# Spreading VectorE's work over ScalarE, GpSimd and TensorE, and giving 160 rows of w2 to five DMA engines

## The chip, the core and the metric

The kernel runs on one core of a Trainium2 chip. The metric is the device time of one execution in microseconds; the median of three runs before the change is 344.48 us (344.46 to 344.8).

## What is computed

One decode step for two sequences: an attention block and a small feed-forward block on the same input, mixed by a gate.

```python
g = sigmoid((x * gate_w).sum(-1, keepdims=True))          # x: [2, 1, 512]
q = (x @ wq)                                              # 32 heads of 128
scores = einsum("bhqd,bhkd->bhqk", q, k_cache) * 128**-0.5  # k_cache: [2, 32, 4096, 128]
o = einsum("bhqk,bhkd->bhqd", softmax(scores), v_cache)
a = o.reshape(2, 1, 4096) @ wo                            # wo: [4096, 512]
b = relu(x @ w1) @ w2                                     # w1: [512, 1376], w2: [1376, 512]
out = g * a + (1 - g) * b
```

Everything is bf16. The two caches are 67 MB each, all inputs together 145.4 MB, and each byte is read once.

## The kernel before

SBUF holds three regions of 8 MB (`kv`, NREG = 3). K and V are each cut into eight units of 8 MB, eight heads of one sequence to a unit. The list `order` gives the order in which units are loaded: K0 to K4, V0, K5, V1, K6, V2, K7, then V3 to V7. Unit n goes into region n modulo 3, so its transfer waits until the unit three places earlier has been used (`freed`). All big transfers are issued by SyncE (SP) in this order (L216 to L242): wq and w1 first, into the third region, then the units, then the two halves of wo (L232) and the four parts of w2 (w2a L236; w2b, w2c, w2d L239), and at last the output. V7 comes in two parts, v7a and v7b. x and gate_w are loaded on ScalarE's queue. A transfer over 128 rows of SBUF is split over sixteen DMA engines, eight rows each; each engine counts the transfer's semaphore up by one when its part has landed, and the waiting engine waits for sixteen.

Each compute engine has a list of operations written out by hand (`_Prog`), and a marker (`signal`) per operation that others can wait for (`waits`). For each K unit VectorE turns the unit in 32 x 32 blocks, in four steps (`k_turn`, L360), and TensorE then multiplies it, 64 matmuls in four steps `rp`, with a padded copy of q (`wz`, written by `w_block` on ScalarE, L351) into four PSUM banks (`k_scores`, L365 and L393). After four units one sequence's scores are complete: VectorE takes the maximum (`sm_max`, L399 to L410), ScalarE the exponentials (`sm_exp`, L414), VectorE turns them (`sm_turn`, L422). For each V unit GpSimd spreads the probabilities into `ptm` (`spread`, L431), TensorE multiplies them with the unit (`v_unit`, 64 matmuls, L448), VectorE masks the result and sums its four column blocks (`v_extract`, L455 and L459), and TensorE adds it into the sequence's output (`v_gather`, L464). `o_denominator` (L470, L473), `o_scale` (L476) and `o_place` (L484, L489) finish the attention; `project` (L500) multiplies it with wo and the hidden layer with w2, in steps of four matmuls in the order in which the weights land, and two engines copy the result out of PSUM (L510).

The gate, the projection of q and the hidden layer h (`gate`, `q_proj`, `ffn_h`, L281 to L343) run at the start, while K0 is being loaded.

## Time and profile before

| | before |
|---|---|
| median of 3 runs | 344.48 us |
| the profiled execution: its own time, its span | 344.46 us, 343.1 us |
| DMA: bytes, mean rate over the span | 145.59 MB, 424 GB/s |
| TensorE matmuls busy | 179.8 us (52%) |
| VectorE busy | 169.7 us (49%) |
| GpSimd busy, ScalarE busy | 35.5 us (10%), 13.5 us (4%) |
| chain that ended last, by engine | DMA 57%, VectorE 24%, TensorE 9%, issue 4% |

The span is the stretch that the profile covers; the execution's own time is 1.36 us longer. Rows of the profile count from the span's start. A group's row gives the line, the engine, the operation, its tiles, how often it ran, and then its busy time and the mean duration of one. PE is TensorE, DVE VectorE, ACT ScalarE, POOL GpSimd, SPq the queue of SyncE. A row of the chain gives start, length and what it was. The trace also holds a record of each DMA packet (start, duration, bytes, queue), but not which of the sixteen engines moved it.

### The profile page before, as it was taken

What the parts mean: (1) busy time and instruction counts of PE and PEld (TensorE: products, weight loads), DVE (VectorE), ACT (ScalarE), POOL (GpSimd) and SP (SyncE); (2) the same over time, 40 slices, a digit from 0 to 9 for tenths busy, and PEclk for the clock granted to TensorE, in tenths of its full rate; (3) what the DMA queues carried; (4) which work ended last, traced back from release to release, by engine and by line L of the source; (5) the groups of instructions that cost most, each with busy time, mean ns of one, the idle gap of its engine ahead of it and who ended that gap; (6) DMA issues with size and microseconds to landing.
All of it is one profiled execution on the core that took longest, in us unless ns stands there. A gap on an engine that the chain in (4) does not pass through costs nothing.

```text
span 343.1 us, 2541 instructions
## 1 busy us (share of the span) xinstructions
PE 179.8 (52%) x1322; PEld 39.6 (12%) x938; DVE 169.7 (49%) x87; ACT 13.5 (4%) x44; POOL 35.5 (10%) x50
## 2 busy tenths in 40 slices
PE   0510196996869409935980099205970503307353
PEld 0210000100001000120120011100020201102122
DVE  0210797979899489439910694219935020102020
ACT  1010001000010110000000000000020000000000
POOL 3000000000000040040013000400004040403100
PEclk9965599899989957995995579955996575856586
DMA  8998989999999989898999989999999999999995
GB/s 325 451 483 374 481 374 481 397 458 420 435 460 390 489 382 474 382 468 390 466 466 391 481 384 466 405 451 405 460 405 443 466 392 474 413 401 449 395 428 216
DMA packets 3588, 145.59 MB, mean 424 GB/s; under 512 B 405, under 2 KB 634, under 8 KB 890
## 3 DMA queue, kind: packets, MB, share of 16 engines
q1 hardware_dynamic: 3572, 145.43, 98.5%
q8 instruction: 9, 0.15, 0.2%
q10 hardware_dynamic: 6, 0.00, 0.0%
q14 instruction: 1, 0.01, 0.0%
HBM read 145.43 MB, written 0.00 MB: 424 GB/s over the span
## 4 chain that ended last, share of the span: by engine, by line
DMA 57%; DVE 24%; PE 9%; issue 4%; another core or an unknown queue 3%; SPq 1%; ACT 1%
DMA kv<-in_A_k_cache_dram 34%; DVE kv L360 22%; DMA kv<-in_B_w_dram 13%; DMA kv<-in_A_v_cache_dram 11%; PE PS L365 4%; PE PS L448 4%; PE PS L393 2%; DVE E L422 1%; ACT E L414 1%; DVE mpad L399 1%; DVE X L459 0%; SPq L232 0%; DVE X L455 0%; PE PS L500 0%
## 5 line engine op out<-in xcount | busy, mean ns | idle before, releaser
L360 DVE STREAM_TRANSPOSE kv<-kv 128x4096 uint32<-128x4096 uint32 x32 | 139.3, 4412 | 50.2 <-DMA kv<-in_A_k_cache_dram 50.2
L365 PE MATMUL PS<-kv,wz 128*128 128x512 bf16 x384 | 114.0, 407 | 0.0
L393 PE MATMUL PS<-kv,wz 128*128 128x512 bf16 x128 | 52.9, 413 | 94.5 <-DVE kv L360 94.4
L431 POOL TENSOR_TENSOR ptm<-E,mask 128x512 bf16<-128x512 bf16 x32 | 32.2, 1039 | 282.2 <-DVE E L422 158.5
L448 PE MATMUL PS<-kv,ptm 128*32 128x512 bf16 x512 | 38.6, 462 | 36.3 <-DMA kv<-in_A_v_cache_dram 36.3
L455 DVE TENSOR_TENSOR X<-PS,maskc 128x512 f32<-128x512 f32 x8 | 5.5, 687 | 79.4 <-PE PS L448 79.4
L393 PEld LDWEIGHTS PS<-kv,wz 128*128 128x128 bf16 x128 | 13.0, 102 | 206.2 <-DVE kv L360 120.6
L448 PEld LDWEIGHTS PS<-kv,ptm 128*32 128x32 bf16 x512 | 17.5, 113 | 54.3 <-issue 47.2
L351 ACT ACTIVATE wz<-q_sb 32x8 bf16<-32x8 bf16 x32 | 6.9, 214 | 154.5 <-PE PS L365 145.6
L464 PE MATMUL PS<-X,selx 128*32 128x128 f32 x16 | 3.5, 302 | 13.3 <-DVE X L459 13.3
L459 DVE TENSOR_REDUCE X<-X 128x128 f32<-128x512 f32 x8 | 8.2, 1024 | 0.3
L399 DVE TENSOR_REDUCE mpad<-PS 128x2 f32<-128x2048 f32 x2 | 4.6, 2292 | 7.5 <-PE PS L365 7.5
L414 ACT ACTIVATE E<-PS,negm 128x1024 bf16<-128x1024 f32 x4 | 4.4, 1109 | 81.8 <-DVE negm L410 81.8
L422 DVE STREAM_TRANSPOSE E<-E 128x2048 bf16<-128x2048 bf16 x2 | 4.6, 2312 | 4.7 <-ACT E L414 4.7
L312 PE MATMUL PS<-kv,xT 128*32 128x512 bf16 x32 | 3.6, 629 | 3.6 <-DMA kv<-in_A_wq_dram 3.6
L500 PE MATMUL PS<-kv,oW 128*2 128x128 bf16 x128 | 2.9, 264 | 4.5 <-DMA kv<-in_A_wo_dram 4.5
L510 DVE CAST ptm<-PS 2x128 bf16<-2x128 f32 x2 | 0.6, 280 | 9.1 <-PE PS L500 9.1
L319 DVE STREAM_TRANSPOSE ptm<-PS 128x1024 f32<-128x1024 f32 x1 | 1.3, 1251 | 6.3 <-PE PS L312 6.3
L286 DVE COPY xT<-PS 128x8 bf16<-128x8 bf16 x1 | 0.2, 164 | 8.1 <-PE PS L284 8.1
L510 ACT ACTIVATE ptm<-PS 2x128 bf16<-2x128 f32 x2 | 0.5, 270 | 84.0 <-PE PS L500 84.0
L464 PEld LDWEIGHTS PS<-X,selx 128*32 128x32 f32 x16 | 1.1, 112 | 19.0 <-DVE X L459 15.7
L500 PEld LDWEIGHTS PS<-kv,oW 128*2 128x2 bf16 x128 | 2.5, 102 | 4.8 <-DMA kv<-in_A_wo_dram 4.2
(56 smaller groups left out, 24.2 us busy)
## 6 DMA issues: line engine op xcount, KB each, us to landing
kv<-in_A_v_cache_dram SPq DMA_DIRECT2D x1, 6144.0 KB, 47.8
kv<-in_A_wq_dram SPq DMA_DIRECT2D x1, 4096.0 KB, 12.2
kv<-in_A_wo_dram SPq DMA_DIRECT2D x2, 2048.0 KB, 40.1
kv<-in_A_v_cache_dram SPq DMA_DIRECT2D x1, 2048.0 KB, 52.3
kv<-in_B_w_dram SPq DMA_DIRECT2D x1, 1376.0 KB, 15.0
kv<-in_B_w_dram SPq DMA_DIRECT2D x1, 640.0 KB, 43.4
kv<-in_B_w_dram SPq DMA_DIRECT2D x1, 512.0 KB, 44.2
kv<-in_A_k_cache_dram SPq DMA_DIRECT2D x8, 40.2
```

Source lines behind the costliest of these rows:

```text
L351: act(lambda e, a=a: e.activation(out=wz[32 * a:32 * a + 32, u % 2, :, 31 + 32 * a:33 + 32 * a], in_=q_sb[32 * a:32 * a + 32, b, ub].rearr ...
L360: dve(lambda v, rp=rp: v.transpose(out=reg[:, 4096 * rp:4096 * (rp + 1)], in_=reg[:, 4096 * rp:4096 * (rp + 1)]), dwaits=([landed(what)] i ...
L365: return e.add_instruction(mybir.InstMatmult(name=nc.get_next_instruction_name(), engine=mybir.EngineType.PE, ins=[e.lower_ap(rhs), e.lowe ...
L393: return e.matmul(dst, lhsT=w, rhs=m, start=first, stop=final, skip_group_check=True)
L399: dve(lambda v: v.tensor_reduce(out=mpad[:, 0:2], in_=PSF[:, 0:2048].rearrange("p (x h q) -> p h x q", h=2, q=16), axis=AX.XY, op=ALU.max) ...
L414: act(lambda a, h=h: a.activation(out=E[:].rearrange("p (x h q) -> p h x q", h=2, q=16)[:, h], in_=PSF[:, 0:2048].rearrange("p (x h q) -> ...
L422: dve(lambda v: v.transpose(out=E[:], in_=E[:]), waits=[f"act_exp{b}"], signal=f"dve_et{b}")
L431: pool(lambda g, src=src, dst=dst: g.tensor_tensor(out=dst, in0=src, in1=msk, op=ALU.mult), waits=([f"dve_et{b}", "dve_mask8"] + ([f"pe_v_ ...
L448: pe(lambda e, ci=ci, t=t: e.matmul(psf(32 * t, 32 * t + 32, c0, 512), lhsT=ptm[:, ci].rearrange("p c h -> p (c h)"), rhs=rows[:, 512 * ci ...
L455: dve(lambda e: e.tensor_tensor(out=X2[:].rearrange("p (c d) -> p c d", c=4), in0=psf(0, 128, c0, 512).rearrange("p (c d) -> p c d", c=4), ...
L459: dve(lambda e: e.tensor_reduce(out=X3[:], in_=X2[:].rearrange("p (c d) -> p d c", c=4), axis=AX.X, op=ALU.add), waits=[f"dve_x_{v}"] + ([ ...
L500: pe(lambda e, t=t, n=n, w=w, m=m: e.matmul(psf(32 * t, 32 * t + 2, FIN_C0, 128), lhsT=w, rhs=m[:, 128 * t:128 * t + 128], start=(n == 0), ...
```

## The change

1. The rows of w2 are dealt anew. 160 rows (`w2p`) are loaded by eight transfers of five SBUF rows each, 4 KB a row, issued ahead of wo (the change's own words put them on the DMA engines 0 to 4); w2a has 64 rows instead of 96, w2b 640 as before, w2c 384 instead of 512, w2d 128 as before. The hidden layer is cut to match, in 14 blocks instead of 11.
2. Work moves off VectorE. To ScalarE: the copies of x and q, parts of the gate, relu of h, the scaling of the maximum, the copy of V's products out of PSUM (except for V7), the last copy of the attention's output. To GpSimd: the mask on V's products, and `w_block`, now one multiplication instead of four ScalarE activations per unit. To TensorE: the gate's product, and the sum over V's four column blocks: `v_gather` takes 512 columns and adds all units of a sequence, and VectorE sums the four blocks once per sequence in `o_scale`.
3. A K unit is turned in two steps instead of four. The first half of K4 is turned ahead of the first softmax, the second half behind it.
4. GpSimd clears one tile (`zero`) instead of eight, the masks are made in fewer steps, `o_denominator` runs once for both sequences.
5. The first half of wo is multiplied by 32 matmuls of 64 x 256 instead of 64 of 2 x 128.

In the built programs VectorE has 44 instructions instead of 109, ScalarE 32 instead of 47, GpSimd 65 as before, SyncE 38 instead of 30.

```diff
-    w2_sb = kv[:, WO, 16384:22016].rearrange("p (r n) -> p r n", n=512)
-
-    act(lambda e: e.dma_start(x_sb, A_x.rearrange("b s d -> (b s) d")).then_inc(sem["x"], 16))
-    act(lambda e: e.dma_start(gw_sb, gate_w.rearrange("(o d) -> o d", o=1)).then_inc(sem["gw"], 16))
+    w2_sb = kv[:, WO, 16384:23552].rearrange("p (r n) -> p r n", n=512)
+    W2 = (("w2p", 0, 4, 0, 40), ("w2a", 160, 1, 4, 64), ("w2b", 224, 5, 5, 128), ("w2c", 864, 3, 10, 128), ("w2d", 1248, 1, 13, 128))
...
+    for j in range(8):
+        sp(lambda e, j=j: e.dma_start(w2_sb[j:40:8, 0:4, :].rearrange("p r n -> p (r n)"),
+                                      B_w2[0:160, :].rearrange("(p r) n -> p (r n)", r=4)[j::8]).then_inc(sem["w2p"], 16),
+           waits=([freed(order[wo_reg - NREG])] if j == 0 else []))
     for x in range(2):
         sp(lambda e, x=x: e.dma_start(wo_sb[:, x * 8192:(x + 1) * 8192],
                                       A_wo[x * 2048:(x + 1) * 2048, :].rearrange("(p r) n -> p (r n)", p=128))
-           .then_inc(sem[f"wo{x}"], 16), waits=([freed(order[wo_reg - NREG])] if x == 0 else []))
-
-    sp(lambda e: e.dma_start(w2_sb[0:96, 10, :], B_w2[1280:1376, :]).then_inc(sem["w2a"], 16))
-    W2 = (("w2b", 0, 5, 0), ("w2c", 640, 4, 5), ("w2d", 1152, 1, 9))
-    for name, row, n, r0 in W2:
+           .then_inc(sem[f"wo{x}"], 16))
+
+    sp(lambda e: e.dma_start(w2_sb[0:64, 4, :], B_w2[160:224, :]).then_inc(sem["w2a"], 16))
+    for name, row, n, r0, _ in W2[2:]:
         sp(lambda e, name=name, row=row, n=n, r0=r0: e.dma_start(
             w2_sb[:, r0:r0 + n, :].rearrange("p r n -> p (r n)"),
             B_w2[row:row + 128 * n, :].rearrange("(p r) n -> p (r n)", p=128)).then_inc(sem[name], 16))
...
-        dve(lambda v: v.tensor_copy(out=xT[:], in_=PSB[0:128, XT_B0:XT_B0 + 8].rearrange("p (t b) -> p t b", t=4)),
-            waits=["pe_xT"], signal="dve_xT0")
-        dve(lambda v: v.tensor_copy(out=xT32[:, :, 0:2], in_=PSB[0:128, XT_B0:XT_B0 + 8].rearrange("p (t b) -> p t b", t=4)),
-            waits=["c_x32"], signal="dve_x32")
...
-        dve(lambda v: v.tensor_tensor(out=xg[:], in0=xT[:], in1=gwT[:].unsqueeze(2).to_broadcast([128, 4, 2]), op=ALU.mult),
-            waits=["dve_xT"], signal="dve_xg")
-        dve(lambda v: v.tensor_reduce(out=xgs[:], in_=xg[:].rearrange("p t b -> p b t"), axis=AX.X, op=ALU.add),
-            waits=["dve_xg"], signal="dve_xgs")
-        pe(lambda e: e.matmul(psf(0, 128, G_C0, 2), lhsT=ones, rhs=xgs[:, :], start=True, stop=True),
-           waits=["dve_xgs", "c_ones"], signal="pe_z")
+            pe(lambda e, t=t: e.matmul(psf(0, 128, G_C0, 2), lhsT=xT32[:, t, 2:3].to_broadcast([128, 128]), rhs=xT32[:, t, 0:2],
+                                       start=(t == 0), stop=(t == 3)),
+               waits=(["act_xT"] if t == 0 else []), signal=("pe_z" if t == 3 else None))
...
-        dve(lambda v: v.tensor_copy(out=q_sb[:].rearrange("p b u h k -> p b (u h k)"),
-                                    in_=qt.rearrange("p (n x) -> p x n", x=32)[:, 0:2]),
-            waits=["dve_qt"], signal="dve_q")
+        act(lambda a: a.activation(out=q_sb[:].rearrange("p b u h k -> p b (u h k)"),
+                                   in_=qt.rearrange("p (n x) -> p x n", x=32)[:, 0:2], func=ACT.Copy),
+            waits=["dve_qt"], signal="act_q")
...
-            dve(lambda v, b=b: v.tensor_scalar(out=hT[:, 0:10, b], in0=PSF[:, H_C0 + b:H_C0 + 20:2], scalar1=0.0,
-                                               scalar2=gm[:, b:b + 1], op0=ALU.max, op1=ALU.mult),
-                waits=["pe_h", "dve_gm"])
-            dve(lambda v, b=b: v.tensor_scalar(out=hT[0:96, 10, b:b + 1], in0=psf(0, 96, H_C0 + 20 + b, 1), scalar1=0.0,
-                                               scalar2=gm[0:96, b:b + 1], op0=ALU.max, op1=ALU.mult),
-                signal=f"dve_h{b}")
+            act(lambda a, b=b: a.activation(out=hT[:, :, b], in_=PSF[:, H_C0 + b:H_C0 + 2 * NF:2], func=ACT.Relu,
+                                            scale=gm[:, b:b + 1]),
+                waits=["pe_h"] + ([] if b else ["act_gm"]), signal=f"act_h{b}")
...
-        for a in range(4):
-            act(lambda e, a=a: e.activation(out=wz[32 * a:32 * a + 32, u % 2, :, 31 + 32 * a:33 + 32 * a],
-                                            in_=q_sb[32 * a:32 * a + 32, b, ub].rearrange("p h k -> p k h"), func=ACT.Copy),
-                 waits=((["dve_q", "c_wz"] if u < 2 else [f"pe_sc_{u - 2}"]) if a == 0 else []),
...
+        out = wz[:, u % 2].rearrange("p k c -> p k c")[:, :, 31:159].rearrange("p k (a x) -> p k a x", a=4)[:, :, :, 0:2]
+        q = q_sb[:, b, ub].rearrange("p h k -> p k h").unsqueeze(2).to_broadcast([128, 4, 4, 2])
+        msk = mask4[:].unsqueeze(1).unsqueeze(3).to_broadcast([128, 4, 4, 2])
+        pool(lambda g: g.tensor_tensor(out=out, in0=q, in1=msk, op=ALU.mult),
+             waits=([["act_q", "dve_mask8"], []] + [[f"pe_sc_{x}"] for x in range(6)])[u], signal=f"pool_wz{u}")
...
-        for rp in range(4):
-            dve(lambda v, rp=rp: v.transpose(out=reg[:, 4096 * rp:4096 * (rp + 1)], in_=reg[:, 4096 * rp:4096 * (rp + 1)]),
-                dwaits=([landed(what)] if rp == 0 else []), signal=f"dve_kt_{u}_{rp}")
+        for h in halves:
+            dve(lambda v, h=h: v.transpose(out=reg[:, 8192 * h:8192 * (h + 1)], in_=reg[:, 8192 * h:8192 * (h + 1)]),
+                dwaits=([landed(what)] if h == 0 else []), signal=f"dve_kt_{u}_{h}")
...
-                    if blk == 0 and rb == 0:
-                        waits = [f"dve_kt_{u}_{rp}"]
+                    if blk == 0 and rb == 0 and rp % 2 == 0:
+                        waits = [f"dve_kt_{u}_{rp // 2}"]
                         if rp == 0:
-                            waits += [f"act_wz{u}"] + (["act_exp0"] if u == 4 else [])
+                            waits += [f"pool_wz{u}"] + (["act_exp0"] if u == 4 else [])
...
-        dve(lambda v: v.tensor_scalar(out=nrow[:].rearrange("p (u r h) -> p u r h", r=4, h=2),
-                                      in0=mmax[:].rearrange("p (u h) -> p u h", h=2).unsqueeze(2).to_broadcast([128, 4, 4, 2]),
-                                      scalar1=-INV_SQRT_DH, scalar2=None, op0=ALU.mult),
-            waits=[f"dve_mm{b}"], signal=f"dve_mn{b}")
-        dve(lambda v: v.transpose(out=negm[:, b, :], in_=nrow[:]), waits=[f"dve_mn{b}"], signal=f"dve_neg{b}")
+        act(lambda a: a.activation(out=nrow[:].rearrange("p (u r h) -> p u r h", r=4, h=2),
+                                   in_=mmax[:].rearrange("p (u h) -> p u h", h=2).unsqueeze(2).to_broadcast([128, 4, 4, 2]),
+                                   func=ACT.Copy, scale=-INV_SQRT_DH),
+            waits=[f"dve_mm{b}"], signal=f"act_mn{b}")
+        dve(lambda v: v.transpose(out=negm[:, b, :], in_=nrow[:]), waits=[f"act_mn{b}"], signal=f"dve_neg{b}")
...
-        dve(lambda e: e.tensor_tensor(out=X2[:].rearrange("p (c d) -> p c d", c=4),
-                                      in0=psf(0, 128, c0, 512).rearrange("p (c d) -> p c d", c=4),
-                                      in1=maskc[:].unsqueeze(2).to_broadcast([128, 4, 128]), op=ALU.mult),
-            waits=[f"pe_v_{v}"] + ([f"dve_y_{v - 1}"] if v else []), signal=f"dve_x_{v}")
-        dve(lambda e: e.tensor_reduce(out=X3[:], in_=X2[:].rearrange("p (c d) -> p d c", c=4), axis=AX.X, op=ALU.add),
-            waits=[f"dve_x_{v}"] + ([f"pe_g_{v - 1}"] if v else []), signal=f"dve_y_{v}")
...
+        if v == 7:
+            dve(lambda e: e.tensor_tensor(out=X, in0=src.rearrange("p (c d) -> p c d", c=4), in1=msk, op=ALU.mult),
+                waits=[f"pe_v_{v}"], signal=f"dve_x_{v}")
+            return
+        act(lambda e: e.activation(out=X2[:], in_=src, func=ACT.Copy), waits=[f"pe_v_{v}"], signal=f"act_x_{v}")
+        pool(lambda e: e.tensor_tensor(out=X, in0=X, in1=msk, op=ALU.mult),
+             waits=[f"act_x_{v}"] + ([] if v else ["dve_setup"]), signal=f"pool_x_{v}")
 
     def v_gather(v):
         b, ub = divmod(v, 4)
-        pe(lambda e: e.matmul(psf(0, 32, O_C0, 128), lhsT=selx[:, 24 - 8 * ub:56 - 8 * ub], rhs=X3[:],
+        pe(lambda e: e.matmul(psf(0, 32, O_C0, 512), lhsT=selx[:, 24 - 8 * ub:56 - 8 * ub], rhs=X2[:],
                               start=(ub == 0), stop=(ub == 3), skip_group_check=True),
-           waits=[f"dve_y_{v}", "dve_selx"] + (["dve_O0"] if v == 4 else ["dve_h1"] if v == 0 else []), signal=f"pe_g_{v}")
...
-    def o_denominator(b):
-        for h in range(2):
-            pe(lambda e, h=h: e.matmul(psf(0, 32, L_C0 + b, 1), lhsT=sell[:, h, :], rhs=lsum[:, b, h:h + 1],
-                                       start=(h == 0), stop=(h == 1), skip_group_check=True),
...
+    def o_denominator():
+        for b in range(2):
+            for h in range(2):
+                pe(lambda e, b=b, h=h: e.matmul(psf(0, 32, L_C0 + b, 1), lhsT=sell[:, h, :], rhs=lsum[:, b, h:h + 1],
+                                                start=(h == 0), stop=(h == 1), skip_group_check=True),
+                   waits=(["act_exp1", "dve_setup"] if b == 0 and h == 0 else []), signal=("pe_l" if b and h else None))
+        dve(lambda v: v.reciprocal(out=rinv[:], in_=psf(0, 32, L_C0, 2)), waits=["pe_l"], signal="dve_rinv")
 
     def o_scale(b):
-        dve(lambda v: v.tensor_scalar(out=O_sb[:, b, :], in0=psf(0, 32, O_C0, 128), scalar1=rinv[:, b:b + 1],
+        dve(lambda v: v.tensor_reduce(out=Osum[:], in_=psf(0, 32, O_C0, 512).rearrange("p (c d) -> p d c", c=4), axis=AX.X, op=ALU.add),
+            waits=[f"pe_g_{4 * b + 3}"], signal=f"dve_S{b}")
+        dve(lambda v: v.tensor_scalar(out=O_sb[:, b, :], in0=Osum[:], scalar1=rinv[:, b:b + 1],
                                       scalar2=gb[0:32, b:b + 1], op0=ALU.mult, op1=ALU.mult),
-            waits=[f"pe_g_{4 * b + 3}", f"dve_rinv{b}", "dve_g"], signal=f"dve_O{b}")
+            waits=[f"dve_S{b}"], signal=f"dve_O{b}")
...
-        dve(lambda v: v.tensor_copy(out=oW[:].rearrange("p (x r) c -> p x r c", x=2),
-                                    in_=psf(0, 128, R_C0, 64).rearrange("p (x b r) -> p x r b", x=2, b=2)),
-            waits=["pe_R"], signal="dve_oW")
+
+        R = psf(0, 128, R_C0, 64).rearrange("p (x b r) -> p x r b", x=2, b=2)
+        act(lambda a: a.activation(out=oW[:, 0:2], in_=R[:, 0:1].to_broadcast([128, 2, 16, 2]), func=ACT.Copy), waits=["pe_R"])
+        act(lambda a: a.activation(out=oW[:, 2], in_=R[:, 1], func=ACT.Copy), signal="act_oW")
...
-        steps = [(oW[:, r, :], wo_sb[:, r * 512:(r + 1) * 512]) for r in range(32)]
-        steps += [(hT[0:96, 10, :], w2_sb[0:96, 10, :])] + [(hT[:, r, :], w2_sb[:, r, :]) for r in range(10)]
-        lands = {0: "wo0", 16: "wo1", 32: "w2a", 33: "w2b", 38: "w2c", 42: "w2d"}
+        for r in range(16):
+            for g in range(2):
+                pe(lambda e, r=r, g=g: e.matmul(
+                    psf(64 * g, 64 * g + 64, FIN_C0 + 256 * g, 256),
+                    lhsT=oW[:].rearrange("p k r c -> p (k r c)")[:, 2 * r:2 * r + 64],
+                    rhs=wo_sb[:, r * 512 + 256 * g:r * 512 + 256 * g + 256], start=(r == 0), stop=False,
+                    tile_position=(0, 64 * g), skip_group_check=True),
+                   dwaits=([(sem["wo0"], 16)] if r == 0 and g == 0 else []),
+                   waits=(["act_oW", "act_h1", "act_exp1"] if r == 0 and g == 0 else []))
+        steps = [(hT[0:40, r, :], w2_sb[0:40, r, :]) for r in range(4)]
+        steps += [(oW[:, 2, r, :], wo_sb[:, 8192 + r * 512:8704 + r * 512]) for r in range(16)]
+        steps += [(hT[0:64, 4, :], w2_sb[0:64, 4, :])] + [(hT[:, r, :], w2_sb[:, r, :]) for r in range(5, NF)]
+        lands = {0: ("w2p", 128), 4: ("wo1", 16), 20: ("w2a", 16), 21: ("w2b", 16), 26: ("w2c", 16), 29: ("w2d", 16)}
         for n, (w, m) in enumerate(steps):
             for t in range(4):
-                pe(lambda e, t=t, n=n, w=w, m=m: e.matmul(psf(32 * t, 32 * t + 2, FIN_C0, 128), lhsT=w, rhs=m[:, 128 * t:128 * t + 128],
-                                                          start=(n == 0), stop=(n == len(steps) - 1), tile_position=(0, 32 * t),
-                                                          skip_group_check=True),
-                   dwaits=([(sem[lands[n]], 16)] if n in lands and t == 0 else []),
-                   waits=(["dve_oW", "dve_h1", "act_exp1"] if n == 0 and t == 0 else []),
+                pe(lambda e, t=t, n=n, w=w, m=m: e.matmul(psf(32 * t, 32 * t + 2, FIN_C0 + 128 * t, 128), lhsT=w,
+                                                          rhs=m[:, 128 * t:128 * t + 128], start=False, stop=(n == len(steps) - 1),
+                                                          tile_position=(0, 32 * t), skip_group_check=True),
+                   dwaits=([(sem[lands[n][0]], lands[n][1])] if n in lands and t == 0 else []),
                    signal=("pe_fin" if n == len(steps) - 1 and t == 3 else None))
...
+    k_turn(4, (0,))
     sm_max(0)
     sm_exp(0)
     sm_turn(0)
     spread(0)
-    k_turn(4)
+    k_turn(4, (1,))
     k_scores(4)
...
-    o_denominator(0)
     w_block(6)
     for v in range(8):
         v_unit(v)
+        if v == 3:
+            o_denominator()
...
-            o_denominator(1)
             o_scale(0)
...
```

## Prediction

> **What bounds the kernel now.** I read the page's row of DMA use first, then its rows of DMA queues, then the chain of waits from its end, then the trace's DMA packet records.

> ```profile
> DMA  8998989999999989898999989999999999999995
> ```
> ```profile
> q1 hardware_dynamic: 3572, 145.43, 98.5%
> q8 instruction: 9, 0.15, 0.2%
> ...
> q14 instruction: 1, 0.01, 0.0%
> ```
> ```profile
> 296.49 44.17 DMA kv<-in_B_w_dram
> 340.66 0.04 issue
> 340.71 0.64 PE PS L500 x18
> 341.35 0.02 issue
> 341.37 0.28 DVE ptm L510
> ```

> The sixteen DMA engines are never idle, and the chain ends on the last transfers of w2. So VectorE (49% of the span) and TensorE (52%) set nothing as long as no transfer is issued late; the end is set by the DMA engine that finishes last. The packet records give it: on one engine each packet starts 3 or 4 ns before the one ahead ends, so they string into sixteen chains without a hole from 1.77 us on. Seven chains end at 338.73 to 339.12, one at 339.90, eight at 340.20 to 340.57. All carry the same bytes. What differs is the 10 instruction packets of the second fence. Each of the eight late chains holds one 16 KB packet of q8 (22.9 to 336.4 us; the ninth comes at 340.45, behind all data): it takes 1.02 us and the data packet behind it 0.49 us longer than its like, 1.5 us in all. The chain of 339.90 holds q14's 8 KB packet (182.51 us; 0.30 and 0.65 us). TensorE starts 258 instructions on average from one q8 packet to the next, 64 bytes each, so q8 is its stream.

> [...]

> **w2 on five engines: the only part on the path.** An engine's share of w2 today is 6 packets of 1 KB (w2a), 8 of 5 KB (w2b), 8 of 4 KB (w2c), 8 of 1 KB (w2d). It becomes 4, 8, 8 of 3 KB, 8. In these chains 1 KB packets follow each other every 42.5 ns and 4 KB packets every 156 ns, so a KB more in a packet is 38 ns, and a 3 KB packet, which no row shows, lies between them at 118. Gone from every engine: 2 x 0.0425 + 8 x 0.038 = 0.39 us. Five engines get 8 packets of 4 KB and eight semaphore writes of 6 ns: 1.25 + 0.05 = 1.30, net +0.91.

> - An engine with a fetch: 340.57 - 0.39 = 340.18 at the latest.
> - One of the five, without a fetch: 339.12 + 0.91 = 340.03 at the latest.

> If the five are among the seven early ones, the last packet comes 0.39 us sooner. Behind it nothing changes: w2d lands 0.42 us after its last packet (340.99), its four matmuls end at 341.35, then two casts and the 2 KB write. w2c has 12 matmuls where it had 16.

> Are they among the seven? A row of x goes to each of two engines, and gate_w, one row, to one of these. The packets put the second of them into an early chain to the end; the first is lost where chains coincide within 1 ns. Eight fetches struck eight different engines, which drawing at random would do 1 time in 8, so they go in turn. If eight neighbours of sixteen take them and the second engine (number 1, if the two are 0 and 1) is free, four of the eight possible stretches leave 0 to 4 free; a turn over the upper eight alone, which eight fetches use up exactly, would leave them free too. So I put it somewhat above half.

> **VectorE's instructions.** Removed from it: 16 of 32 K turns (two of twice the size cost the same 17.4 us), gate, h, q and mask operations at 0.15 to 0.23 each, 8 reductions L459 (1.02) and 7 multiplications L455 (0.69). VectorE was not the bound, so this time is worth nothing. But in the built programs it falls from 109 instructions to 44, and q14's packet came with its 62nd, the 41st of GpSimd, the 16th of SP. If it is VectorE's, it goes; worth 0.95 us to an engine that is not last, hence nothing unless it is one of the five.

> **What is new on the waits.** All of this is costed at nothing; here is the cover.

> - K turns by halves: TensorE starts a half 4.4 us later and has 32 matmuls instead of 16 behind the last turn, 7.0 us for 3.5 (112.44 to 116.12 today). Each score unit ends 3.5 us later, and so does the issue that waits for it. Most issues have 12 to 31 us of queued transfers ahead of them. The tightest:

> ```profile
> 145.06 0.33 SPq L229 DMA_DIRECT2D kv<-in_A_v_cache_dram  x1
> ```

>   It waits for K unit 4. After the change: K4 lands at 114.44, half a turn ends at 123.3, softmax takes its 7.9 us (116.12 to 124.02 today) and 0.1 for ScalarE's step in it: 131.3; the other half 140.1; 32 matmuls 147.1. K5's first engine lands at 151.37, and 1.0 us goes from issue to first packet (wq: 0.74, 1.77), so the queue runs dry only from 150.4: 3.3 us to spare. After an idle stretch TensorE's first twelve matmuls stand 0.43 apart instead of 0.217 (from 128.41), which costs 2.6 of the 3.3 at most.
> - wz blocks on GpSimd: one multiplication instead of four activations (0.21 each). Nearest rows: 0.12 (small memset) to 1.04 (L431, sixteen times the elements); I take 0.2. They queue ahead of spread and behind score units that are done earlier; TensorE has two units in hand.
> - V's extract: a ScalarE copy of 512 columns (half of the 1.11 for 1024 at L414: 0.55) and a GpSimd multiplication (1.04 at L431 for as many elements; in f32 up to twice that) ahead of spread: 1.6 to 2.7 us on spread(7), which then ends at 320.4 to 321.5 (318.76 today), while v7a lands at 322.59; I take the lower, by the row of the same count.
> - Gather over 512 columns instead of 128: 0.41 becomes about 1.1. At the end: V7 done 328.65, multiplication 329.4, gather 330.5, reduction (1.02) 331.6, scale 332.0, place 332.6, ScalarE twice 333.2 where oW stood at 332.23. Then 32 matmuls of twice the width, 1.1 to 2.1 us: 335.3, while wo1 lands at 337.54. 2.2 us of cover; without it the end would move one for one.
> - SP issues eight more transfers at 0.43, 3.4 us, ahead of wo. wo0 was issued at 294.70 with 30.7 us queued.

> **Sum.** The profiled execution took 344.46 (span 343.1); 344.46 - 0.39 = 344.07; the median of the runs is 0.02 higher: 344.1.

> **Rivals.**
> 1. Slower: one or more of engines 0 to 4 takes a fetch. Then it ends at 340.20 to 340.57 plus 0.91, 0.54 to 0.91 later than today: 345.0 to 345.4, with several struck the upper end. It decides from the first of the five struck. Against it: the second engine's early chain. For it: nothing in the records names the other four. Chance 0.30.
> 2. The refill of q14 is not VectorE's, or is not lost, and falls to one of the five: 339.90 + 0.91 = 340.81, 0.24 later: 344.7. Chance 0.07.
> 3. The issue of V1 comes after 150.4. With all 32 matmuls at 0.43 (13.7 us) unit 4 ends at 153.8 and the end moves by 3.4: 347.9. Against it: from 133.2 they stand 0.217 apart. Chance 0.05.
> 4. The transfers don't go to five engines. All on one: 40 x 0.156 = 6.2, 339.1 - 0.4 + 6.3 = 345.0, 4.4 late: 348.9. Over all sixteen: nothing gained, 344.5. x's two rows took two engines, gate_w's row one, so five rows on five is the reading of the rows. Chance 0.03.
> 5. More than forecast. If no fetch delays an engine, the five end last, at 340.03, 0.54 sooner: 343.9. If the delays fall so that all sixteen end level, they end at the mean of today's ends, 339.69, 0.87 sooner: 343.6. Against it: all eight chains with a fetch are late. Chance of the two 0.08. [...]

> [...]

> **Numbers.** Forecast 0.47, own range 343.9 to 344.3 (late chains differ by 0.37 among themselves). The range must reach rival 1: 343.7 to 345.4; rivals 3, 4 and part of 5 are left out. 0.2% is 0.69 us, about what a measurement of this kernel can tell from no change. The forecast lies within it, but for 0.05; with rival 5 faster is 0.13. Slower: 0.25 of rival 1 and 0.05 of 3 and 4: 0.30. The rest, 0.57, is the same.

> **What would show it.** Right: five chains end near 339.7 to 340.0, the rest at or before 340.2, w2d's landing near 340.6, no q14 packet between 0 and 340 us. Wrong: a chain with eight packets of 4 KB and a fetch, ending after 341; a hole in the chains near 150 us; the projection's matmuls still behind when w2d lands.

## The result: 0.15% slower, and the profile after

| | before | after |
|---|---|---|
| median of 22 runs each, us | 344.59 (344.32 to 344.80) | 345.09 (344.92 to 345.39) |
| ratio, 95% interval | | 1.0015 [1.0009, 1.0022] |
| profiled execution, us (span) | 344.46 (343.1) | 345.29 (343.9) |
| VectorE busy, us | 169.7 | 155.5 |
| GpSimd busy, us | 35.5 | 43.2 |

The kernel became slower by 0.5 us where 0.4 us less was forecast. The two profiled executions lie 0.83 us apart: after's is 0.2 us above its median and before's 0.13 below, so about 0.3 of the 0.83 belong to these two executions.

The page of after, its row of DMA use and its DMA queues:

```profile
DMA  8998989899998989899998999999898999999996
...
q1 hardware_dynamic: 3620, 145.43, 98.6%
q8 instruction: 9, 0.15, 0.2%
```

There is no row of q14 any more: the 8 KB instruction refill at 182.51 us is gone from the data's way. The end of the chain of waits of after (start, us, what):

```profile
302.85 38.60 DMA kv<-in_B_w_dram
341.45 0.04 issue
341.49 0.64 PE PS L495 x16
342.13 0.02 issue
342.15 0.28 DVE ptm L504
```

The end has the same form as before: it waits for w2's last transfers, which land 0.79 us later. (This chain row ends at w2c. The last write of w2d's semaphore comes at 341.78, against 340.99 before.) What follows the landing still takes 0.64 and 0.28 us. So the engines that took over VectorE's work are not what is late. The DMA engines are.

The packet records, strung into sixteen chains as in the prediction, show where. The five chains with the eight 4 KB packets end at 340.81 to 340.96, and none of them holds a fetch of q8, one of the 16 KB instruction packets. (In before TensorE starts 258 instructions on average from one of them to the next, 63.5 bytes of packet to an instruction; no record names the engine, so that q8 is TensorE's stream, and its instructions 64 bytes each, is an estimate from these numbers.) Of the other eleven, the three without a fetch end at 339.46 to 339.65, the eight with one at 340.82 to 341.32. From 10 to 325 us little differs: a chain without a fetch loses 0.3 to 0.75 us there in all, in before 0.3 to 0.65. But between 325 and 328.8 us, while the 4 KB packets run, the packets of all sixteen are long. The eleven have only full 16 KB packets there, and each chain loses 0.92 to 0.97 us against its usual 615 ns a packet. In before, the same stretch costs between -0.01 and 0. The view of busy time by stretches shows it; the last two columns are DMA share and GB/s. First before, then after:

```profile
core 0: us, PE busy (x) PEld busy (x) DVE busy (x) ACT busy (x) POOL busy (x), PEclk, DMA share, GB/s
322.00:325.00 3.00, 2.28 (x24) 1.06 (x28) 0.00 (x0) 0.00 (x0) 0.00 (x0) 0.50 0.99 421
325.00:328.80 3.80, 3.66 (x48) 1.33 (x36) 0.09 (x1) 0.00 (x0) 0.00 (x0) 0.68 1.01 431
```

```profile
322.00:325.00 3.00, 2.00 (x20) 0.89 (x24) 0.00 (x0) 0.00 (x0) 0.00 (x0) 0.50 1.03 437
325.00:328.80 3.80, 3.12 (x36) 1.19 (x32) 0.00 (x0) 0.00 (x0) 0.00 (x0) 0.66 0.99 310
```

The DMA share is 0.99 in after, against 1.01 in before: the engines are busy, and yet they move 310 GB/s instead of 431. The busy share doesn't show this. The bytes moved, and the time of a packet of known size, do. In the records' bins of half a microsecond the low point is 245 GB/s; in the worst bins the 4 KB packets take 1.8 times their 159 ns on average, and the 16 KB packets of the other engines 1.8 times their 615.

The sum nearly closes: the latest chain 340.57, less the 0.39 us of removed packets, plus 0.93 gives 341.11. It ended at 341.32, 0.21 later, in this execution, which lies 0.2 us above the median.

So the question is what makes eight small transfers on five engines slow down all sixteen. Four things about them are new: they run on five engines, they are many, they read 160 rows of w2 with a stride, and they write SBUF rows eight apart. In the first expectations S stands for the source's stride, D for the destination rows, N for the number of the transfers and their semaphores.

### The profile page after: what moved, and what is told of

Same layout as the page of the kernel before. It is cut to its first block, busy times and chain, and to the rows that moved or that the text cites. A ratio compares the mean times of both kernels' runs of the same rounds, so it can differ in the third digit from the quotient of the medians.

```text
span 343.9 us, 2454 instructions
## 1 busy us (share of the span) xinstructions
PE 186.6 (54%) x1312; PEld 39.5 (11%) x928; DVE 155.5 (45%) x42; ACT 12.8 (4%) x29; POOL 43.2 (13%) x55
## 3 DMA queue, kind: packets, MB, share of 16 engines
q1 hardware_dynamic: 3620, 145.43, 98.6%
HBM read 145.43 MB, written 0.00 MB: 423 GB/s over the span
## 4 chain that ended last, share of the span: by engine, by line
DMA 64%; PE 20%; DVE 13%; SPq 2%; issue 0%
DMA kv<-in_A_k_cache_dram 44%; DVE kv L335 13%; PE PS L340 12%; DMA kv<-in_B_w_dram 11%; DMA kv<-in_A_v_cache_dram 9%; PE PS L368 4%; PE PS L423 3%; SPq L230 2%; SPq L234 0%; PE PS L495 0%; SPq L240 0%; DVE ptm L504 0%; PE PS L443 0%; SPq L238 0%; SPq L214 0%
## 5 line engine op out<-in xcount | busy, mean ns | idle before, releaser
L335 DVE STREAM_TRANSPOSE kv<-kv 128x8192 uint32<-128x8192 uint32 x16 | 138.5, 8691 | 84.0 <-DMA kv<-in_A_k_cache_dram 84.0
L340 PE MATMUL PS<-kv,zero 128*128 128x512 bf16 x384 | 114.9, 410 | 0.0
L368 PE MATMUL PS<-kv,zero 128*128 128x512 bf16 x128 | 53.1, 415 | 98.2 <-DVE kv L335 88.9
L368 PEld LDWEIGHTS PS<-kv,zero 128*128 128x128 bf16 x128 | 13.2, 103 | 209.4 <-issue 108.7
L434 DVE TENSOR_TENSOR X<-PS,maskc 128x512 f32<-128x512 f32 x1 | 0.7, 692 | 63.0 <-PE PS L423 63.0
L438 POOL TENSOR_TENSOR X<-X,maskc 128x512 f32<-128x512 f32 x7 | 7.3, 1039 | 114.4 <-ACT X L437 114.4
L443 PE MATMUL PS<-X,zero 128*32 128x512 f32 x16 | 8.4, 604 | 7.4 <-POOL X L438 6.6
L437 ACT ACTIVATE X<-PS 128x512 f32<-128x512 f32 x7 | 4.2, 596 | 142.0 <-PE PS L423 142.0
L374 DVE TENSOR_REDUCE zero<-PS 128x2 f32<-128x2048 f32 x2 | 4.5, 2271 | 8.4 <-PE PS L340 8.4
L293 PE MATMUL PS<-kv,zero 128*32 128x512 bf16 x32 | 3.6, 629 | 4.3 <-DMA kv<-in_A_wq_dram 4.3
L482 PE MATMUL PS<-kv,oW 128*64 128x256 bf16 x32 | 3.0, 363 | 0.4 <-ACT oW L475 0.4
```

Source lines behind the costliest of these rows:

```text
L335: dve(lambda v, h=h: v.transpose(out=reg[:, 8192 * h:8192 * (h + 1)], in_=reg[:, 8192 * h:8192 * (h + 1)]), dwaits=([landed(what)] if h == ...
L340: return e.add_instruction(mybir.InstMatmult(name=nc.get_next_instruction_name(), engine=mybir.EngineType.PE, ins=[e.lower_ap(rhs), e.lowe ...
L368: return e.matmul(dst, lhsT=w, rhs=m, start=first, stop=final, skip_group_check=True)
L374: dve(lambda v: v.tensor_reduce(out=mpad[:, 0:2], in_=PSF[:, 0:2048].rearrange("p (x h q) -> p h x q", h=2, q=16), axis=AX.XY, op=ALU.max) ...
L437: act(lambda e: e.activation(out=X2[:], in_=src, func=ACT.Copy), waits=[f"pe_v_{v}"], signal=f"act_x_{v}")
L438: pool(lambda e: e.tensor_tensor(out=X, in0=X, in1=msk, op=ALU.mult), waits=[f"act_x_{v}"] + ([] if v else ["dve_setup"]), signal=f"pool_x ...
```

## Experiments

All were timed beside the kernel before, and each ratio is to it. The lines shown for each are its row for 325 to 328.8 us in the view of busy time by stretches, with DMA share and GB/s as the last two columns. "Lost per chain" is worked out from the packet records as above, for chains that hold no dealt packet.

### Source stride, destination rows of another stride, or the number of engines

Three kernels that change the row numbers of the eight transfers: both sides to five neighbours, the source alone, the destination alone. The diff of the first, which holds the other two:

```diff
-        sp(lambda e, j=j: e.dma_start(w2_sb[j:40:8, 0:4, :].rearrange("p r n -> p (r n)"),
-                                      B_w2[0:160, :].rearrange("(p r) n -> p (r n)", r=4)[j::8]).then_inc(sem["w2p"], 16),
+        sp(lambda e, j=j: e.dma_start(w2_sb[5 * j:5 * j + 5, 0:4, :].rearrange("p r n -> p (r n)"),
+                                      B_w2[0:160, :].rearrange("(p r) n -> p (r n)", r=4)[5 * j:5 * j + 5]).then_inc(sem["w2p"], 16),
```

In the second and third one side keeps its old rows, so w2's rows meet the wrong hidden units.

> The j-th of the eight w2p transfers takes five neighbouring 4 KB rows of w2 (20 KB in a piece) into five neighbouring SBUF rows, instead of every eighth row into every eighth row. Theory S (source: five engines reading w2 in step at addresses 32 KB apart slow all sixteen): the slow stretch at 325 to 328.8 us goes, its 0.93 us per chain with it, and the time is the forecast's, 344.1 to 344.3. Theory D (destination: five engines writing SBUF rows of other engines): rows are still not the engines' own, 345.0 to 345.2; gone only if the distance of eight rows matters. Theory N (number: forty semaphore writes between 4 KB packets): nothing changes, 345.1.

> Only the source is changed: five neighbouring 4 KB rows of w2, still into every eighth SBUF row (so these 160 rows meet the hidden values of other rows). Theory S: 344.1 to 344.3, no slow stretch. Theories D and N: 345.1, the stretch stays at 0.9 us per chain.

> Only the destination is changed: every eighth 4 KB row of w2 into five neighbouring SBUF rows (these 160 rows meet the hidden values of other rows). Theory S: 345.1, the stretch stays. Theory D: the stretch shrinks or goes, 344.1 to 344.6. Theory N: 345.1.

Measured: 344.92 us, ratio 1.0007 [0.9998, 1.0016]; 345.22, 1.0016 [1.0008, 1.0025]; 344.98, 1.0010 [1.0002, 1.0019]. The slow stretch is in all three:

```profile
325.00:328.80 3.80, 3.29 (x40) 1.20 (x36) 0.00 (x0) 0.00 (x0) 0.00 (x0) 0.64 1.05 341
```

```profile
325.00:328.80 3.80, 2.54 (x36) 1.00 (x32) 0.00 (x0) 0.00 (x0) 0.00 (x0) 0.81 1.01 310
```

```profile
325.00:328.80 3.80, 2.94 (x40) 1.15 (x36) 0.00 (x0) 0.00 (x0) 0.00 (x0) 0.80 1.03 346
```

The stride of the source is not it. Other destination rows raise the rate from 310 to 341 and 346, but don't mend it (0.87 to 0.93 us lost per chain in the first kernel, 0.74 to 0.81 in the third). That left D open, since neighbouring rows need not be the right ones.

The fourth gives the 160 rows to all sixteen engines, as one transfer of 32 SBUF rows of 5 KB:

```diff
-    for j in range(8):
-        sp(lambda e, j=j: e.dma_start(w2_sb[j:40:8, 0:4, :].rearrange("p r n -> p (r n)"),
...
+    sp(lambda e: e.dma_start(w2_sb[0:32, 0:5, :].rearrange("p r n -> p (r n)"),
+                             B_w2[0:160, :].rearrange("(p r) n -> p (r n)", r=5)).then_inc(sem["w2p"], 16),
```

> The changed kernel with the 160 rows in one transfer of 32 SBUF rows of 5 KB over all sixteen engines (15 blocks of the hidden layer instead of 14): everything but the five engines' share stays. If the rest of the change is worth nothing, as forecast, this is the time of the kernel before, 344.5 to 344.7, all chains as in its trace but without q14's packet, and no slow stretch. If VectorE's thinner program, the half turns or TensorE's longer sums cost or gain on their own, it differs from that: a rival in which they, and not the w2p transfers, made the changed kernel slower gives 345.1.

Measured: 345.60 us, 1.0027 [1.0017, 1.0036], the slowest of all and over both times that I expected.

```profile
325.00:328.80 3.80, 2.94 (x40) 1.13 (x36) 0.00 (x0) 0.00 (x0) 0.00 (x0) 0.76 1.02 319
```

One transfer on sixteen engines with one semaphore has the stretch too, 0.94 to 1.3 us on every chain. So neither the number of transfers nor the five engines make it. What this one has in common with the eight is that its rows are not all 128.

### Where the rows lie: the engines' own rows

Theory D was put in a form that runs can test. The SBUF rows are counted in groups of four neighbours, group i, counted from 0, being rows 4i to 4i+3. The theory takes group i for engine i's own, the one that it writes in transfers over all 128 rows, and says that an engine that writes another's group slows the rest. The packet records name neither engine nor row: that the i-th row of a small transfer falls to engine i, and that group i is its own, are assumptions, and no run shows them one by one. Under them engines 0 to 3 write, in each of after's first four transfers, the groups 0, 2, 4 and 6. Its new rival H was that a small region of HBM, read by few engines, is slow.

**Own rows.** The same 160 rows on the same five engines, as four transfers of five 8 KB rows, the i-th row of each in rows 4i to 4i+3, so that under D each engine writes its own group:

```diff
-        sp(lambda e, j=j: e.dma_start(w2_sb[j:40:8, 0:4, :].rearrange("p r n -> p (r n)"),
-                                      B_w2[0:160, :].rearrange("(p r) n -> p (r n)", r=4)[j::8]).then_inc(sem["w2p"], 16),
+        sp(lambda e, j=j: e.dma_start(w2_sb[j:20:4, 0:8, :].rearrange("p r n -> p (r n)"),
+                                      B_w2[0:160, :].rearrange("(p r) n -> p (r n)", r=8)[j::4]).then_inc(sem["w2p"], 16),
```

> The same 160 rows on the same five engines, as four transfers of five 8 KB rows; each SBUF row is now one of the four that stand 4i to 4i+3 for engine i, rows 0 to 19 (in after, rows 0 to 39, eight apart from transfer to transfer). Theory D (an engine that writes SBUF rows other than those it writes in a transfer over all 128 rows slows all sixteen): the slow stretch at 325 to 328.8 us is gone, from 0.93 us per chain to under 0.1, the end comes 0.8 to 0.9 earlier than after, about 344.2. Theory H (a small stretch of HBM, 160 KB, read by few engines at once is slow): the stretch stays at 0.8 to 1.0 per chain, about 345.1. A fetch that falls on one of the five engines would add about 0.9 in either case and shows as a second late group.

Measured: 344.29 us, 0.9989 [0.9980, 0.9998].

```profile
325.00:328.80 3.80, 3.80 (x48) 1.48 (x40) 0.00 (x0) 0.00 (x0) 0.00 (x0) 0.66 0.99 418
```

The stretch is gone: 0.00 to 0.01 us lost on each of the sixteen chains, and 8 KB packets take 310 ns. The end of its chain of waits:

```profile
300.00 40.47 DMA kv<-in_B_w_dram
340.47 0.04 issue
340.52 0.62 PE PS L495 x16
```

The wait ends at 340.47 instead of 341.45. No fetch fell on the five.

**Another source.** After, with the small transfers reading the K cache, rows 12.3 MB apart, in place of w2:

```diff
-                                      B_w2[0:160, :].rearrange("(p r) n -> p (r n)", r=4)[j::8]).then_inc(sem["w2p"], 16),
+                                      A_k_cache.rearrange("b h (s r) d -> (b h s) (r d)", r=16)[37 * j:37 * j + 12005:3001])
+           .then_inc(sem["w2p"], 16),
```

> After, but the eight small transfers read rows of the K cache that lie 12.3 MB apart in place of w2's first 160 rows (so the product leaves out w2's first 160 rows); destination, sizes and number as in after. Theory H (the small source region is slow): the slow stretch at 325 to 328.8 us is gone, about 344.2 to 344.3. Theory D (the destination rows): it stays at 0.8 to 1.0 us per chain, about 345.1.

Measured: 345.24 us, 1.0017 [1.0008, 1.0025], and 0.94 to 1.05 us lost per chain.

```profile
325.00:328.80 3.80, 3.36 (x36) 1.21 (x32) 0.00 (x0) 0.00 (x0) 0.00 (x0) 0.50 0.98 306
```

The source has nothing to do with it. H falls.

**The same packets, other rows.** Own rows differs from after in the size and number of its transfers as well. So the same four transfers into the same twenty SBUF rows, but transfer j fills rows 5j to 5j+4; under D the first of them sends four engines into group 0:

```diff
-        sp(lambda e, j=j: e.dma_start(w2_sb[j:20:4, 0:8, :].rearrange("p r n -> p (r n)"),
-                                      B_w2[0:160, :].rearrange("(p r) n -> p (r n)", r=8)[j::4]).then_inc(sem["w2p"], 16),
+        sp(lambda e, j=j: e.dma_start(w2_sb[5 * j:5 * j + 5, 0:8, :].rearrange("p r n -> p (r n)"),
+                                      B_w2[0:160, :].rearrange("(p r) n -> p (r n)", r=8)[5 * j:5 * j + 5]).then_inc(sem["w2p"], 16),
```

> [...] Theory D (whose rows are written decides): the slow stretch at 325 to 328 us is back, 0.6 to 1.0 us per chain, about 344.9 to 345.2. Rival (four transfers of 8 KB in place of eight of 4 KB took the stretch away): no stretch, about 344.3.

Measured: 345.18 us, 1.0019 [1.0010, 1.0028]. The profiled execution loses 1.49 to 1.52 us on each of the eleven; at 345.85 it lies 0.67 us above the median, so the usual loss is smaller, by estimate some 0.8 us (1.50 - 0.67):

```profile
325.00:328.80 3.80, 2.34 (x32) 0.86 (x24) 0.00 (x0) 0.00 (x0) 0.00 (x0) 0.82 1.03 263
```

Nothing but the rows that each transfer brings together is different from own rows (w2's rows go along with it, and the source is ruled out above), and the rate goes from 418 GB/s, with rows four apart, to 263, with neighbours. So that is the cause; that it acts through which engine writes which rows is D's reading of it.

**Foreign, but one writer more.** Own rows moved by four, so that under D engine i writes group i+1. Only group 5 then has two engines that write it: engine 5, whose 16 KB packets go on, and engine 4, which writes into it meanwhile. (The product still reads rows 0 to 19, so w2's first 160 rows enter it wrongly.)

```diff
-        sp(lambda e, j=j: e.dma_start(w2_sb[j:20:4, 0:8, :].rearrange("p r n -> p (r n)"),
+        sp(lambda e, j=j: e.dma_start(w2_sb[4 + j:24:4, 0:8, :].rearrange("p r n -> p (r n)"),
```

> [...] Theory D1 (any foreign row slows): the stretch is back, 0.6 to 1.0 us per chain, about 345. Theory D2 (only several engines in one group slow each other): no stretch or under 0.2 per chain, about 344.3.

Measured: 345.16 us, 1.0014 [1.0005, 1.0023]: the time of D1, but for a reason nearer to D2.

```profile
325.00:328.80 3.80, 2.71 (x36) 1.02 (x32) 0.00 (x0) 0.00 (x0) 0.00 (x0) 0.77 1.00 392
```

The chains tell the two apart. Two of them lose 1.03 and 1.20 us, one with the 8 KB packets (against the 310 ns that such a packet takes with own rows) and one without. The other four with 8 KB packets lose 0.15 to 0.20, though under D all wrote foreign rows, and the remaining ten, which wrote none, lose 0.14 to 0.17. So writing a foreign row cost no more than that here. What is left is that two engines in one group share what one usually has to itself. By estimate the size fits: engine 4 puts 4 x 8 KB into the group, and 32 KB at 16 KB in 0.615 us are 1.23 us; while two share the group, each should lose about that, and the two lost 1.03 and 1.20. That this other chain is engine 5's is inferred from its loss. It also holds a fetch, ends last at 341.19 and sets this kernel's time.

### The rest of the change, by itself

The rest of the change, with w2's first 224 rows as one transfer over all 128 SBUF rows and one over 96, as before has the latter:

```diff
+    sp(lambda e: e.dma_start(w2_sb[:, 0, :], B_w2[0:128, :]).then_inc(sem["w2p"], 16),
+       waits=[freed(order[wo_reg - NREG])])
...
+    sp(lambda e: e.dma_start(w2_sb[0:96, 1, :], B_w2[128:224, :]).then_inc(sem["w2a"], 16))
```

> The rest of the change, with w2's first 224 rows as one transfer over all 128 SBUF rows (1 KB each, before wo) and one of 96 rows (as before has it, after wo): no transfer on five engines. Theory D: no dip at 325 us (under 0.1 us per chain), every engine carries before's bytes, about 344.6 to 344.8, that is before's time within 0.2. Theory H (small source): the dip stays, over 0.5 us per chain, about 345.2. If instead something else in the change (ScalarE's and GpSimd's share) costs time, it shows here as time over before without a dip.

Measured: 344.62 us, 1.0000 [0.9991, 1.0009].

```profile
325.00:328.80 3.80, 3.80 (x41) 1.51 (x36) 0.00 (x0) 0.00 (x0) 0.00 (x0) 0.53 1.01 418
```

The rest of the change, which takes VectorE from 109 instructions to 44, is worth nothing that could be measured here, neither gain nor loss (the interval reaches 0.3 us either way). No stretch, 0.02 to 0.04 us lost per chain.

### Towards a faster kernel

**Eight engines.** The rest of the change, with 224 rows dealt to engines 0 to 7 as four transfers of eight 7 KB rows, own rows, and no 64-row or 96-row transfer:

```diff
+        sp(lambda e, j=j: e.dma_start(w2_sb[j:32:4, 0:7, :].rearrange("p r n -> p (r n)"),
+                                      B_w2[0:224, :].rearrange("(p r) n -> p (r n)", r=7)[j::4]).then_inc(sem["w2p"], 16),
...
-    sp(lambda e: e.dma_start(w2_sb[0:64, 4, :], B_w2[160:224, :]).then_inc(sem["w2a"], 16))
```

> The rest of the change, with w2's first 224 rows on eight engines (0 to 7) as four transfers of eight 7 KB rows, each in the SBUF rows 4i to 4i+3 of its engine, and no 96-row transfer: eight engines lose 14 packets of 1 KB (0.6 us), eight gain 14. Theory D: no dip at 325 us. If all fetches of TensorE's instructions stay off engines 0 to 7, the late chains end about 0.6 us earlier than in before and the end is near 343.9 to 344.1; if one falls on engines 5 to 7, that chain ends about 0.6 later than in before, near 345.2. Theory H: dip of 0.5 us or more in any case, 344.6 at best.

Measured: 344.56 us, 0.9999 [0.9990, 1.0007].

```profile
325.00:328.80 3.80, 3.69 (x48) 1.34 (x40) 0.00 (x0) 0.00 (x0) 0.00 (x0) 0.75 1.00 423
```

Two of the eight took a fetch (one of them at 336.49 us) and end last, at 340.21 and 340.50; the six others of the eight end by 339.19, the fetched ones of the rest by 339.91. The 345.2 that I expected for that case left out what this kernel gives back elsewhere: before loses 0.27 to 0.38 us after 328.8 us on every chain without a late fetch, this one 0.01 to 0.05. That loss lies at the 96-row transfer (64 rows in after), and goes with it. It makes up about half of the 0.64 us by which the expectation was off; the rest was not traced.

**Five engines, 44 rows each.** So the dealing should stay on engines 0 to 4 and be larger, and the 64-row transfer should go:

```diff
+        sp(lambda e, j=j: e.dma_start(w2_sb[j:20:4, 0:11, :].rearrange("p r n -> p (r n)"),
+                                      B_w2[0:220, :].rearrange("(p r) n -> p (r n)", r=11)[j::4]).then_inc(sem["w2p"], 16),
...
+    sp(lambda e: e.dma_start(w2_sb[0:4, 11, :], B_w2[220:224, :]).then_inc(sem["w2a"], 16))
```

> The rest of the change, with 44 rows of w2 on each of engines 0 to 4 as four transfers of five 11 KB rows into own rows, and four single rows in place of the 64-row transfer. Theory D: no slow stretch at 325 us and none at 335 to 337.5 us; the other eleven chains carry 14 KB less than in before (-0.6 us) and miss the late stretch (-0.25): late ends near 339.8; the five carry 30 KB more (+1.3) and end near 339.7 to 340.0. End about 343.8, against 344.6 for before. If one of the five takes a fetch of TensorE's: about 345.2. If the late stretch has nothing to do with the 64-row or 96-row transfer: about 344.1.

Measured: 343.75 us (343.58 to 343.87), 0.9972 [0.9961, 0.9982]: faster than both kernels, 0.9 us under before.

```profile
325.00:328.80 3.80, 3.55 (x48) 1.23 (x36) 0.20 (x1) 0.00 (x0) 0.00 (x0) 0.71 1.00 426
```

```profile
298.06 39.22 DMA kv<-in_A_wo_dram
337.28 0.04 issue
337.33 2.64 PE PS L496 x87
339.97 0.02 issue
339.99 0.62 PE PS L496 x16
```

The five end at 339.61 to 339.71, the eight with a fetch at 339.19 to 339.69: thirteen of sixteen end within 0.52 us. The chain's last long wait is now for wo's second half, and the projection's matmuls fill the time until w2c has landed at 339.94. DMA engines and TensorE now end nearly together, so more dealing alone would probably not bring much; no run tried it.

**The same in before.** The same dealing, nothing else of the change:

```diff
+    for j in range(4):
+        sp(lambda e, j=j: e.dma_start(w2_sb[j:20:4, 10:21, :].rearrange("p r n -> p (r n)"),
+                                      B_w2[1152:1372, :].rearrange("(p r) n -> p (r n)", r=11)[j::4]).then_inc(sem["w2p"], 16),
...
```

> The same dealing of w2 (44 rows on each of five engines, own rows) in before, with nothing else of the change. If the rest of the change is worth nothing: as the kernel with 44 rows above, 343.8 to 343.9. If the instruction refill at 182 us that before has on the queue q14 falls on one of the five: about 344.5. If the rest of the change was needed for it (VectorE's work in the end stage), the end is later than the last landing by more than in before.

Measured: 344.70 us, 0.9998 [0.9989, 1.0007].

```profile
q14 instruction: 1, 0.01, 0.0%
```

```profile
297.83 40.59 DMA kv<-in_A_wo_dram
338.43 0.04 issue
338.47 3.17 PE PS L508 x100
341.63 0.02 issue
```

The page's row of q14 alone does not tell: the kernel with 44 rows has the same one, for a packet at 342.43 us, behind all data. The packet records do. Here q14's refill is back in the middle of the queue, at 182.66 us, and lies on one of the five: that chain ends at 340.81, alone, where the four others of the five end by 339.89 and no other chain after 339.97. It reaches the end through wo's second half: fifteen of its sixteen parts have landed by 337.56, the last at 338.43, and TensorE's 100 matmuls run without a pause from there to 341.63. So the rest of the change, worth nothing with an even dealing, is worth about 0.9 us with this one: by what it takes out of an instruction stream (the records don't say whose), not by what it takes off VectorE's time.

## Why the prediction was wrong, point by point

- **What bounds the kernel:** right. The last of sixteen full DMA chains sets the end in before, in after and in the experiments; only in the two with 44 rows does TensorE, working without a pause from the landing of wo's second half, come level with it.
- **w2 on five engines:** this is the step that failed. "Five engines get 8 packets of 4 KB and eight semaphore writes of 6 ns: 1.25 + 0.05 = 1.30, net +0.91" and "340.57 - 0.39 = 340.18" price a packet by its size and take it that it costs the other engines nothing. With after's rows, where under D two engines write into one group, both terms are wrong: a 4 KB packet took about 0.23 (median) and up to 0.34 us instead of 0.156, and each of the other eleven engines lost 0.92 to 0.97 us. With own rows the sum holds as it stood: the eight late chains end on average at 339.96, 0.44 sooner than before's 340.39 (forecast 0.39), the five at 339.64, 0.77 later than the early seven's 338.87 (forecast 0.91, for packets of 4 KB), and the kernel takes 344.29 for the 344.1 forecast, 0.35 less than before beside it.
- **The five are free of fetches:** right, in after and in the nine other kernels that deal to five. With eight engines two were struck. Rival 1 did not happen. Its time, 345.0 to 345.4, did, by another mechanism: that the time fell into the range held open for rival 1 is luck, and only the chain ends show that it was not it.
- **Five engines (rival 4):** right. Five chains hold the eight packets of 4 KB.
- **q14's refill:** right that it goes with the change. It was costed at nothing "unless it is one of the five"; the last experiment shows that case, at about 0.9.
- **K turns by halves and V1's issue (rival 3):** right. V1 was issued at 147.17 (forecast 147.1), and no hole opened in the chains.
- **wz, extract, gather:** covered, as forecast. wz's multiplication took 0.25 (0.2), GpSimd's extract 1.04 (the lower row; that f32 could take twice as long was an allowance that no row shows, and this multiplication is in f32), the gather 1.05 (1.1). The projection's 32 wide matmuls took 2.99 us in after (granted clock 0.62), above the 1.1 to 2.1, and 1.94 with own rows (clock 1.00); wo1 hid both.
- **SP's eight issues:** mis-sized, and hidden. They took 0.66 to 0.81 us each, not 0.43; the queue ahead of them lasted until 325 us, as the chain of waits of after shows, where the last of them is followed by 38.60 us of DMA.
- **The rest of the change costed at nothing:** right with an even dealing, by the kernel with full rows: 1.0000 [0.9991, 1.0009].

What was not asked in the prediction is whether it matters which rows a new transfer writes. The bytes per engine were counted, and the rows that they go to were not looked at, because before holds nearly nothing but full transfers. The one exception stood in its trace. The 96-row transfer runs in two bunches, from 335.0 and from 336.3 us, and right behind them the rate falls from 428 to 323 and 322 GB/s (bins of half a microsecond), with 5 KB packets at 1.3 and 1.5 times their usual time. I took that loss, 0.3 us on every chain, as given.

## What to carry to other kernels

When a transfer is dealt to few DMA engines or covers other than all 128 SBUF rows, look at which rows it writes together, and time the choice. Here 160 rows of w2 four SBUF rows apart, from row 0 on, cost 0.00 to 0.01 us per chain (own rows); eight apart, as after has them, they cost 0.92 to 0.97 on chains that moved something else, and into five neighbours 1.49 to 1.52 in the profiled execution. Balance the engines by when each one ends, instruction packets included (1.5 us for one of q8 in before), not by bytes. And judge a full DMA queue by GB/s and by the time of packets of one size: its busy share was 0.99 in after while the rate was 310 GB/s instead of 431.
